# Issuing all output writes of a decode forward-and-backward kernel from SyncE instead of GpSimd

## The chip, the cores and the metric

The kernel runs on one core of a Trainium2 chip. The metric is the device time of one execution in microseconds (us); the engines are named as the profile names them: PE (TensorE matmul), PEld (its weight loads), DVE (VectorE), ACT (ScalarE), POOL (GpSimd) and SP (SyncE). SP computes nothing here; it begins DMA transfers.

## The reference

Two layers, each an attention block over a cached K and V and then an MLP, for one token in each of two batches; then the gradients of nine inputs. Cut to what matters:

```python
def _A_ref(x, k_cache, v_cache, wq, wo):        # x 2x1x1024; caches 2x4x16384x128; 32 query heads
    q = (x @ wq).reshape(B, 1, 32, 128).transpose(0, 2, 1, 3)
    k = jnp.repeat(k_cache, 8, axis=1)
    v = jnp.repeat(v_cache, 8, axis=1)
    p = softmax(einsum("bhqd,bhkd->bhqk", q, k) * 128 ** -0.5)
    return einsum("bhqk,bhkd->bhqd", p, v).transpose(0, 2, 1, 3).reshape(B, 1, 4096) @ wo

def _B_ref(x, w1, b1, w2, b2):                  # w1 1024x3584, w2 3584x1024
    return gelu(layernorm(x) @ w1 + b1) @ w2 + b2

x = A_x
for _ in range(2):
    x = x + _A_ref(layernorm(x), k_cache, v_cache, wq, wo)
    x = x + _B_ref(layernorm(x), w1, b1, w2, b2)
out = x, and the vjp of all this with grad_out: gradients of A_x, k_cache, v_cache, wq, wo, w1, b1, w2, b2
```

All arrays are bf16. The outputs are out_0 (x) and out_1 to out_9 (the gradients); those of the two caches, out_2 and out_3, are 33.5 MB each, and together the outputs are 98.6 MB by the page's account. The two layers share their weights and caches, so each gradient is a sum over both layers.

## The kernel before, in words

The kernel goes once forward through both layers and once back, and streams K, V and the weights from HBM again in every pass: two forward passes of attention (`attn_fwd`) with their MLPs, then MLP and attention backward for layer 1, then the same for layer 0. While attention of layer 0 goes backward (`attn_bwd` with `outputs`, from about 765 us on), the kernel also computes and writes all weight and cache gradients, since only then both layers' terms are known.

**Chunks and slots.** Each piece of data of 1 MiB, loaded or to be written, is a `Chunk`. SBUF has 13 slots for them (plus four borrowed from tiles that are no longer or not yet needed, in earlier stages). `Program.emit` records pieces of work with the chunks that they use; `Program.run` then goes through the pieces in order. Ahead of each piece it gives free slots to the next chunks in the order of their first use, and begins a chunk's load at once; after the last piece that uses a chunk its slot is free. So a slot that gets free goes straight to the next chunk, load or output, and its load stands in SP's instructions at that place, with a wait for whatever last used the slot: for a chunk that was written out, the landing of that write.

The order in which the pieces stand is the order of each engine's instructions; nothing is reordered later. The waits are semaphores. DMAs begun by SP take eight completion semaphores in turn, and each waits for the landing of the eighth before it on the same semaphore; POOL's DMAs have eight of their own.

**Attention backward, steps.** A step s handles 1024 columns of V (`kblock`: DVE transposes a quarter of a chunk, L313, PE multiplies it, L326) and, 16 steps later, the same of K (`direct`, L351: 8 matmuls a step, 32 a chunk). A slope is computed on DVE (L804 to L806), exchanged across partitions by ACT (L360), and the weights wo and wq come in as blocks that PE transposes (L288).

**Outputs.** Of these there are four kinds, each of which begins its write from POOL:
- dK and dV (`kv_outputs`): for each of 8 head groups and 4 column chunks, one chunk for dK (w = 0) and one for dV. PE transposes scores into `blk` (L944), and 8 matmuls with `qm` (L962) fill a PSUM bank each; `cast_out` (L180 on ACT, L183 on DVE, chosen by a running account of both) casts each into the chunk; after the eighth, L967 begins the write of 1 MiB. There are 64 of them.
- weight gradients (`dw_units`, `pieces_rows`): matmuls of rows of two vectors (L1001), again cast by `cast_out`, 8 or 7 to a chunk; L1016 begins the write. There are 31 of these, 23 of 1 MiB and 8 of 896 KB.
- two bias gradients (`dbias`, L1034), of 2 and 7 KB.
- out_0 and out_1 (`col_to_row`, L393), of 4 KB each. out_0 is written in the middle, at 701.9 us; out_1 is the last write of the kernel.

The 31 pieces of weight gradients are spread among the steps by a credit that `outputs` keeps; the last eight, of wq, and some of dK and dV are still to be made when the last load has been issued.

Loads are begun by SP: `ld_kv` (L252, K and V) and `ld_rows` (L257, weights). POOL computes `pow` for the layer norms (L413) in the passes before, and begins two small DMAs at the start.

Of the kernel before, what the change touches and what calls it, by code (L numbers as in the profile page):

```python
# [38 lines left out]
class Program:  # L39
# [11 lines left out]
    def emit(self, fn, uses=()):  # L51
        i = len(self.ops)
        self.ops.append((fn, tuple(uses)))
        for c in uses:
            if c.first is None:
                c.first = i
            c.last = i
# [27 lines left out]
def kernel(  # L85
# [24 lines left out]
    nc = tc.nc  # L110
# [3 lines left out]
    GP = nc.gpsimd  # L114
# [36 lines left out]
    def flat(t):  # L151
        return t.rearrange("p a b -> p (a b)")
# [5 lines left out]
    def ob():  # L158
        st["ob"] += 1
        return obanks[st["ob"] % 3]  # L160


    def load_of(engine, us):
        st[engine] += us
        m = min(st["act"], st["dve"])
        st["act"] = min(st["act"] - m, 2.0)
        st["dve"] = min(st["dve"] - m, 2.0)
# [10 lines left out]
    def cast_out(dst, src):  # L178
        if st["act"] <= st["dve"]:
            S.copy(out=dst, in_=src)  # L180
            load_of("act", 0.67)
        else:
            V.tensor_copy(out=dst, in_=src)  # L183
            load_of("dve", 0.68)

    def dve(us):
        load_of("dve", us)
# [30 lines left out]
    def e_of(l, g):  # L218
        return Et[l][:, g * 1024:(g + 1) * 1024].rearrange("p (a h b) -> p a h b", a=NB, h=8)

    def d_of(l, pos, g):
        t = D1t[:, g * 1024:(g + 1) * 1024] if l == 1 else D0t[:, (pos % 2) * 1024:(pos % 2 + 1) * 1024]
        return t.rearrange("p (a h b) -> p a h b", a=NB, h=8)
# [24 lines left out]
    dKv = out_2.rearrange("b h (p t) d -> (b h) p t d", p=128)  # L248
    dVv = out_3.rearrange("b h (p t) d -> (b h) p t d", p=128)
# [133 lines left out]
    def col_to_row(colT, dram_out):  # L383
        c = P.chunk()

        def f():
            row = c.ap[0:2, 0:D]
            for j0 in range(0, DJ, 4):
                ps = ob()[0:2, :].rearrange("p (a b) -> p a b", a=4)
                for j in range(4):  # L390
                    PE.transpose(ps[:, j, :], colT[:, j0 + j, :], identf[:])
                V.tensor_copy(out=row[:, j0 * 128:(j0 + 4) * 128], in_=flat(ps))
            GP.dma_start(dram_out, row)  # L393

        emit(f, [c])

# [509 lines left out]
    def kv_outputs(pos, g):  # L906

        res = []
        qms = {}

        def rows16():
            ps = ob().bitcast(BF16)[0:16, 0:256].rearrange("p (w d) -> p w d", w=2)
            for w in range(2):
                PE.transpose(ps[:, w, :], qd[:, w, g].rearrange("p l r -> p (l r)"), ident[:])
            r16 = small.tile([16, 2, 128], BF16, name="r16", bufs=2)
            V.tensor_copy(out=r16[:], in_=ps)
            dve(0.35)
            qms["r16"] = r16

        def spread(w, t4):  # L920
            def f():
                if t4 == 0:
                    qms[w] = qmp.tile([128, 8, 128], BF16, name=f"qm{w}")
                ps = ob().rearrange("p (t d) -> p t d", t=4)
                for tl in range(4):
                    PE.matmul(ps[:, tl, :], lhsT=sel8[:, t4 * 4 + tl, :], rhs=qms["r16"][:, w, :], start=True,  # L926
                              stop=True)
                cast_out(qms[w][:, t4 * 4:(t4 + 1) * 4, :], ps)
            return f

        res.append((16, rows16, ()))
        for n, (w, t4) in enumerate([(0, 0), (0, 1), (1, 0), (1, 1)]):
            res.append((17 + n, spread(w, t4), ()))
        for n, (c, w) in enumerate([(c, w) for c in range(NCH) for w in range(2)]):
            stg = P.chunk()
            hold = {}

            def turn(c=c, w=w, hold=hold):
                st["tp"] += 1
                tp = tpb[st["tp"] % 2][:].bitcast(BF16)[:, 0:512].rearrange("p (a b) -> p a b", b=128)  # L940
                for bi in range(4):
                    for l in range(2):
                        src = d_of(l, pos, g) if w == 0 else e_of(l, g)
                        PE.transpose(tp[64 * l:64 * l + 64, bi, :],  # L944
                                     src[:, 4 * c + bi].rearrange("p h b -> p (h b)"), ident[:])
                blk = bkp.tile([128, 4, 128], BF16, name="blk")
                src = tp.rearrange("p a (j t) -> p a j t", j=4)
                dst = blk[:].rearrange("p j (a t) -> p a j t", a=4)
                if st["act"] + 0.36 <= st["dve"] + 0.4:
                    S.copy(out=dst.bitcast(I32), in_=src.bitcast(I32))  # L950
                    load_of("act", 0.36)
                else:
                    V.tensor_copy(out=dst, in_=src)
                    dve(0.4)
                hold["blk"] = blk

            res.append((LAG_O + 2 * n - 2, turn, ()))
            for u in range(8):
                def unit(c=c, w=w, u=u, hold=hold, stg=stg):
                    ps = ob()  # L960
                    j = u // 2
                    PE.matmul(ps, lhsT=hold["blk"][:, j, :],  # L962
                              rhs=flat(qms[w][:, (u % 2) * 4:(u % 2) * 4 + 4, :]), start=True, stop=True)
                    cast_out(stg.ap.rearrange("p (s j q d) -> p s q j d", j=4, q=2, d=128)[
                        :, (u % 2) * 2:(u % 2) * 2 + 2, :, j], ps.rearrange("p (s q d) -> p s q d", q=2, d=128))
                    if u == 7:
                        GP.dma_start((dKv if w == 0 else dVv)[g, :, c * 32:(c + 1) * 32, :],  # L967
                                     stg.ap.rearrange("p (t d) -> p t d", d=128))
                res.append((LAG_O + 2 * n + u // 4, unit, [stg]))
        return res  # L970
# [5 lines left out]
    def row_of(name, c0, n):  # L976
        q, off = ROWS[name]
        return rows[32 * q:32 * q + 4, off + c0:off + c0 + n]
# [29 lines left out]
    def pieces_rows(out_ap, n_in, n_out, c0=0):  # L1008

        rb = max(1, CH // n_out)  # L1010
        res = []
        for j0 in range(0, n_in // 128, rb):
            units = [(j0 + j, c0 + c, 512, j * n_out + c) for j in range(rb) for c in range(0, n_out, 512)]

            def store(ap, j0=j0):
                GP.dma_start(out_ap[j0 * 128:(j0 + rb) * 128, c0:c0 + n_out].rearrange("(j p) n -> p j n", p=128),  # L1016
                             ap[:, 0:rb * n_out].rearrange("p (j n) -> p j n", j=rb))

            res.append((units, store))
        return res  # L1020

    def dbias(yn, n, out_ap):
        q, _ = ROWS[yn]
        c = P.chunk()
        res = []
        for c0 in range(0, n, 512):
            def f(c0=c0):
                ps = ob()[0:1, :]
                PE.matmul(ps, lhsT=ones_bf[32 * q:32 * q + 4, 0:1], rhs=row_of(yn, c0, 512), start=True, stop=True,
                          tile_position=(32 * q, 0))  # L1030
                V.tensor_copy(out=c.ap[0:1, c0:c0 + 512], in_=ps)
                dve(0.6)
                if c0 + 512 >= n:
                    GP.dma_start(out_ap.rearrange("(o f) -> o f", o=1), c.ap[0:1, 0:n])  # L1034
            res.append((f, [c]))
        return res

# [199 lines left out]
```

## Time and profile before

| what | us |
|---|---|
| median of 3 runs | 1311.39 (1309.65 to 1316.94) |
| the profiled execution | 1310.87 |
| its span (first to last instruction) | 1309.1 |
| PE busy | 1006.0 (77%) |
| DVE busy | 794.5 (61%) |
| ACT busy | 585.1 (45%) |
| POOL busy | 64.6 (5%) |
| granted TensorE clock, mean of the span | 0.733 |

The DMA queue of SP moved 364.94 MB in 71.9% of the time of the 16 DMA engines, that of POOL 98.66 MB in 18.9%. From issue to landing (median) a 1 MiB load of V took 16.2 us, of K 13.8, a 1 MiB write 6.3.

How to read it: "busy" is the time in which an engine executes; a wait names the line that ended it. A row of a timeline gives start, duration, engine, line, operation and tiles, and in brackets the idle time before it and what ended that. For DMAs the duration is that of the issue alone; the landing is given apart. In a table of stretches each row has the stretch, its length, the busy us of PE, PEld, DVE, ACT and POOL with their numbers of instructions, the granted clock (1.00 is full speed), the DMA engines' mean busy share and the GB/s moved. The clock that the chip grants PE changes between 1.0 and 0.5 every few tens of us in most of the span.

### The profile page before, as it was taken

The numbers are of one execution on the slowest core, as the hardware profiler recorded it, in microseconds if no ns is written. First come the engines' busy times: TensorE is split into PE (matmuls) and PEld (weight loads), VectorE is DVE, ScalarE is ACT, GpSimd is POOL, SyncE is SP. The second block draws the span as 40 slices with busy tenths as digits, with TensorE's granted clock in tenths as the row PEclk, the third lists the DMA queues.
The fourth block names the chain that finished last, engine by engine and source line by source line (L and its number), as shares of the span: only waits on it lengthen the run. The fifth ranks groups of instructions, "written<-read, shape, count | busy, mean of one in ns | idle before, by whom it ended". The sixth has DMA issues, their size and how long they took to land. (4 is left out here: it accounts for less than half of the span.)

```text
span 1309.1 us, 36548 instructions
## 1 busy us (share of the span) xinstructions
PE 1006.0 (77%) x15785; PEld 727.7 (56%) x15785; DVE 794.5 (61%) x1633; ACT 585.1 (45%) x1462; POOL 64.6 (5%) x115
## 2 busy tenths in 40 slices
PE   4656654878756487777669888888898988898987
PEld 4555554867755487776668865444444444344342
DVE  5766651278765126765644476776667667766575
ACT  0312311213232123555443336867666666757554
POOL 0000000000000000000000000110110001101111
PEclk9999999855555557567658977788677667858575
DMA  9999999999999997999999936899898999988856
GB/s 360 414 414 413 414 414 361 320 341 387 413 413 414 409 383 286 365 412 411 415 411 398 399 122 243 333 377 378 343 358 321 346 343 351 362 324 315 302 200 251
DMA packets 100174, 465.93 MB, mean 356 GB/s; under 512 B 7298, under 2 KB 7298, under 8 KB 60844
## 3 DMA queue, kind: packets, MB, share of 16 engines
q1 hardware_dynamic: 83196, 364.94, 71.9%
q0 software_dynamic: 16816, 98.66, 18.9%
q8 instruction: 123, 2.02, 0.6%
q14 instruction: 39, 0.32, 0.1%
HBM read 364.95 MB, written 98.62 MB: 354 GB/s over the span
## 5 line engine op out<-in xcount | busy, mean ns | idle before, releaser
L313 DVE STREAM_TRANSPOSE kT<-slot 128x512 int32<-128x512 int32 x460 | 310.3, 696 | 121.3 <-PE sc L326 111.0
L326 PE MATMUL sc<-qbd,kT 128*128 128x32 bf16 x4096 | 282.7, 230 | 15.5 <-DVE kT L313 11.4
L326 PEld LDWEIGHTS <-kT 128*128 128x128 bf16 x4096 | 223.8, 121 | 72.3 <-issue 45.7
L351 PEld LDWEIGHTS <-slot 128*128 128x128 bf16 x3680 | 152.4, 105 | 131.8 <-issue 53.8
L351 PE MATMUL sb<-xt,slot 128*128 128x8 bf16 x3680 | 168.7, 177 | 62.9 <-DMA slot<-in_A_v_cache_dram 35.5
L180 ACT CAST slot<-sc 128x512 bf16<-128x512 f32 x303 | 173.6, 588 | 89.5 <-PE sc L962 52.1
L172 ACT COPY kT<-tp 128x512 int32<-128x512 int32 (+1 forms) x165 | 95.9, 582 | 196.0 <-PE tp L288 185.6
L288 PE MATMUL tp<-ident,slot 128*128 128x128 bf16 x1832 | 179.3, 258 | 5.3 <-DVE kT L175 2.1
L183 DVE CAST slot<-sc 128x512 bf16<-128x512 f32 x198 | 134.4, 682 | 65.1 <-PE sc L962 34.2
L962 PE MATMUL sc<-qm,blk 128*128 128x512 bf16 x349 | 158.1, 489 | 14.8 <-ACT slot L180 5.8
L288 PEld LDWEIGHTS <-slot 128*128 128x128 bf16 x1832 | 140.5, 116 | 8.9 <-issue 4.2
L360 ACT COPY xt<-ds 32x64 int32<-32x64 int32 x512 | 123.9, 242 | 30.0 <-DVE ds L806 23.5
L527 ACT ACTIVATE e<-sc 128x512 bf16<-128x512 f32 x32 | 19.0, 597 | 233.8 <-DVE sc L524 198.9
L180 ACT CAST slot<-sb 128x512 bf16<-128x512 f32 x141 | 82.8, 587 | 46.3 <-PE sb L962 27.3
L175 DVE COPY kT<-tp 128x1024 bf16<-128x1024 bf16 (+1 forms) x83 | 53.9, 649 | 81.7 <-PE tp L288 68.9
L183 DVE CAST slot<-sb 128x512 bf16<-128x512 f32 x110 | 75.2, 684 | 34.2 <-PE sb L1001 22.7
L1001 PE MATMUL sc<-rows 4*128 4x512 bf16 x152 | 73.7, 507 | 15.2 <-ACT slot L180 12.1
L962 PE MATMUL sb<-qm,blk 128*128 128x512 bf16 x163 | 78.8, 483 | 4.7 <-ACT slot L180 2.1
L360 ACT COPY xt<-e 32x128 int32<-32x128 int32 x256 | 75.6, 295 | 3.9
L962 PEld LDWEIGHTS <-blk 128*128 128x128 bf16 x512 | 40.4, 105 | 64.6 <-issue 59.8
L967 POOL DMA_DIRECT2D out_dram<-slot x64 | 34.1, 533 | 359.3 <-ACT slot L180 168.5
L1001 PE MATMUL sb<-rows 4*128 4x512 bf16 x88 | 44.6, 507 | 6.8 <-ACT slot L180 4.0
(264 smaller groups left out, 906.0 us busy)
## 6 DMA issues: line engine op xcount, KB each, us to landing
slot<-in_A_v_cache_dram SPq DMA_DIRECT2D x110, 1024.0 KB, 16.2
slot<-in_A_k_cache_dram SPq DMA_DIRECT2D x109, 1024.0 KB, 13.8
out_dram<-slot POOLq DMA_DIRECT2D x87, 1024.0 KB, 6.3
slot<-in_A_wq_dram SPq DMA_DIRECT2D x30, 1024.0 KB, 12.9
slot<-in_A_wo_dram SPq DMA_DIRECT2D x30, 1024.0 KB, 16.5
slot<-in_B_w_dram SPq DMA_DIRECT2D x20, 1024.0 KB, 13.2
slot<-in_B_w_dram SPq DMA_DIRECT2D x20, 896.0 KB, 17.4
ds<-in_A_v_cache_dram SPq DMA_DIRECT2D x8, 1024.0 KB, 16.9
```

The costliest lines, as they stand in the source:

```text
L172: S.copy(out=dst.bitcast(I32), in_=src.bitcast(I32))
L175: V.tensor_copy(out=dst, in_=src)
L180: S.copy(out=dst, in_=src)
L183: V.tensor_copy(out=dst, in_=src)
L288: PE.transpose(tp[:, j, :], t, ident[:])
L313: V.transpose(out=kT[:].bitcast(I32).rearrange("p (w j m) -> p w j m", w=4, j=4), in_=c.ap[:, (i % 4) * 1024:(i % 4 + 1) * 1024].bitcast(I ...
L326: PE.matmul(sc[:, a0:a0 + 4, :, 2 * (i % 4) + q], lhsT=kv[:, 2 * q + w, :, e], rhs=qbd[:, g, 2 * w + e], start=(w == 0 and e == 0), stop=( ...
L351: PE.matmul(acc, lhsT=c.ap[:, n * 128:(n + 1) * 128], rhs=xv[:, i // 4, t // 2, :, 2 * (i % 4) + t % 2], start=(i == 0 and t == 0), stop=( ...
L360: S.copy(out=d[32 * t:32 * t + 32, c0:c0 + cn, j, :], in_=s[32 * j:32 * j + 32, c0:c0 + cn, t, :])
L962: PE.matmul(ps, lhsT=hold["blk"][:, j, :], rhs=flat(qms[w][:, (u % 2) * 4:(u % 2) * 4 + 4, :]), start=True, stop=True)
L967: GP.dma_start((dKv if w == 0 else dVv)[g, :, c * 32:(c + 1) * 32, :], stg.ap.rearrange("p (t d) -> p t d", d=128))
L1001: PE.matmul(ps, lhsT=row_of(xn, j * 128, 128), rhs=row_of(yn, c0, cn), start=True, stop=True, tile_position=(32 * q, 0))
```

## The change

Four lines: the queue on which the output writes are begun. Everything else, the order of the pieces included, is as before. POOL keeps the two small DMAs of the start.

```diff
@@ col_to_row
-            GP.dma_start(dram_out, row)
+            nc.sync.dma_start(dram_out, row)
@@ kv_outputs, after the eighth unit
-                        GP.dma_start((dKv if w == 0 else dVv)[g, :, c * 32:(c + 1) * 32, :],
+                        nc.sync.dma_start((dKv if w == 0 else dVv)[g, :, c * 32:(c + 1) * 32, :],
                                      stg.ap.rearrange("p (t d) -> p t d", d=128))
@@ pieces_rows, store
-                GP.dma_start(out_ap[j0 * 128:(j0 + rb) * 128, c0:c0 + n_out].rearrange("(j p) n -> p j n", p=128),
+                nc.sync.dma_start(out_ap[j0 * 128:(j0 + rb) * 128, c0:c0 + n_out].rearrange("(j p) n -> p j n", p=128),
                              ap[:, 0:rb * n_out].rearrange("p (j n) -> p j n", j=rb))
@@ dbias
-                    GP.dma_start(out_ap.rearrange("(o f) -> o f", o=1), c.ap[0:1, 0:n])
+                    nc.sync.dma_start(out_ap.rearrange("(o f) -> o f", o=1), c.ap[0:1, 0:n])
```

## The prediction

> **What bounds the kernel now.** The change touches 99 output writes; all but one (out_0, begun at 701.93) are begun after 791 us, so I read the page, then the stage from 791 to 1304 alone: its busy times, SP's waits, the chain of waits, and the timelines of SP and POOL. First the chain on the page (shares of the span), and two stretches with the busy us of PE, PEld, DVE, ACT and POOL, then granted clock, DMA share, GB/s:
>
> ```profile
> PE 26%; ACT 7%; DVE 4%; DMA 1%; issue 1%; POOL 0%; POOLq 0%; ACTq 0%; DVEq 0%; SPq 0%
> ```
>
> ```profile
> 100.00:200.00 100.00, 60.10 (x1301) 52.16 (x1301) 58.70 (x121) 27.00 (x82) 0.00 (x0) 1.00 1.02 414
> 840.80:1090.90 250.10, 219.25 (x2253) 116.61 (x2252) 171.78 (x313) 170.07 (x389) 25.38 (x46) 0.75 0.93 351
> ```
>
> The chain names the compute engines and gives DMA 1%. But in the 250 us from 840.8 to 1090.9, where loads and writes run together, two things are nearly full: PE (219 of 250 us, 31 us idle) and the DMA engines (0.93). Compute sets the time there, and DMA stands just behind it. The first row is the rate when loads alone run: 414 GB/s, so 1 MiB takes 2.53 us.
>
> What paces the loads in that stretch (SP's waits: us in total, times, longest):
>
> ```profile
> SPq L252 <- DMA out_dram<-slot: 187.5, 24, 14.2
> SPq L257 <- DMA out_dram<-slot: 31.1, 3, 10.6
> ```
>
> SP stands 219 of 250 us waiting for an output write to land, because the next load goes into the slot that the write empties. Meanwhile POOL goes on and begins further writes. SP and POOL in one such place, and the chain of the same place (start, us, what):
>
> ```profile
> 891.84 0.33 SPq L252 DMA_DIRECT2D slot<-in_A_k_cache_dram  x1
> 903.20 0.33 SPq L252 DMA_DIRECT2D slot<-in_A_v_cache_dram  x1
> 907.22 0.33 SPq L252 DMA_DIRECT2D slot<-in_A_k_cache_dram  x1
> ```
>
> ```profile
> 885.58 0.53 POOL L967 DMA_DIRECT2D out_dram<-slot  x1 [6.51 <-DVE do_raw L741]
> 891.16 0.53 POOL L967 DMA_DIRECT2D out_dram<-slot  x1 [5.05 <-ACT slot L180]
> 895.24 0.76 POOL L1016 DMA_DIRECT2D out_dram<-slot  x1 [3.54 <-DVE slot L183]
> 898.01 0.53 POOL L967 DMA_DIRECT2D out_dram<-slot  x1 [2.01 <-ACT kT L172]
> ```
>
> ```profile
> 885.58 6.15 DMA out_dram<-slot
> ...
> 891.84 13.27 DMA slot<-in_A_k_cache_dram
> ```
>
> Each load of the first fence was released by the landing of a write of the second: 885.58 frees the load at 891.84, 891.16 the one at 903.20, 895.24 the one at 907.22. While SP waited, two or three more writes were on their way, so the DMA engines had work. The third fence is the one place of the stretch where the chain runs through DMA: the write takes 6.15 us to land, the load 13.27, and PE's L351 then starts.
>
> **What the change does to the order.** The instruction order of PE, DVE and ACT is the same; POOL loses 99 DMAs and SP goes from 354 to 453. In SP's new order a write stands where its last cast is emitted, and the load into its slot mostly stands right behind it: write 885.58, load 891.84, write 891.16, load 903.20, write 895.24, load 907.22, write 898.01. So the write of 898.01, ready 9.2 us before the load of 907.22, must now wait until that load is issued. Going through the stage with the recorded issue times, 30 of 99 writes have such a later load ahead of them; they come to 97 us, 3.2 us each, before any of it feeds back. No load has a write ahead of it that was issued later than itself, so loads lose nothing directly.
>
> The larger effect is on the DMA engines. When SP waits for the landing of the DMA that it issued last, nothing of its queue is left to move, and POOL's queue, which filled this gap, is gone. What one such gap costs, from transfers that ran alone (a write on POOL near the end, then a load on SP at 769.4; us from issue to landing):
>
> ```profile
> DMA to landing us min/median/max: 4.6/4.6/4.6
> ```
>
> ```profile
> DMA to landing us min/median/max: 5.0/5.0/5.0
> ```
>
> Less the 2.53 us in which 1 MiB moves, that is 2.05 and 2.45 us in which nothing moves. A write on SP is not in this trace, and the gap in question is the end of a write and the start of a load, so I take the middle, 2.25, and keep both ends.
>
> **The sum.** From the load of 840.8 up to the load of 1090.9 SP's new order holds 47 writes and 43 loads, 92.3 MB, and 28 of the loads stand directly behind the write of their own slot.
> - Moving: at the loads-only 414 GB/s 223 us; at the mixed rate of the row above, 351/0.93 = 377, 245 us. One queue is like the first row, half of it writes like the second; I take 400: 231 us.
> - Gaps: 28 x 2.25 = 63 us (57 to 69).
> - Together 294 us for what takes 250 now: 44 us too much (30 to 64).
> - Lead: the stretch's 18 K loads are issued 10.9 to 33.9 us, median 18.3, before the first L351 matmul that reads them (SP's issue against every 32nd L351). A load alone needs 5.0, so 13 us of lateness is used up once, before PE waits (6 at the tightest): 44 - 13 = **31 us**; ends 30 - 13 = 17 and 64 - 6 = 58.
> - Other stages: 11 more such loads, 25 us of gaps, lie before 840 and after 1090.9, where the DMA share is 0.59 (764 to 830) and 0.87 (1090.9 to 1250, 21 us idle). I count them at nothing; uncovered, they are the 25 us.
> - out_0: a 4 KB write at 701.9 that now stands behind four loads (issued 702.0 to 704.6, landing 13.5 to 17.5 us later); the next load, issued at 707.0, waits for it until about 722, one gap of 2.25 us. Its cover is that the first weight block of this stage lands at 694.9 and is read from 700.5, 5.6 us later. Zero; 2 us without that cover.
> - SP issues 99 more DMAs at 0.33 to 0.50 us, 33 to 50 us spread over waits of 219 in the stretch alone: inside them. POOL gets back 0.53 to 0.76 us each and has nothing waiting for it: zero.
> - All DMAs of SP take eight completion semaphores in turn and wait for the landing of the eighth before. Loads and writes now share them; a queue that drains every 90/28 = 3.2 DMAs is never eight deep: zero.
> - The last writes (from 1280.47) have no load between them and land 4.6 us after issue; on SP the issue is shorter by up to 0.4 us: zero.
>
> The profiled execution took 1310.87 us (its span 1309.1 and 1.8 around it), 0.5 under the median of 1311.39. 1310.9 + 31 = 1342.
>
> **Rivals.**
> 1. No change. PE is idle 31 us of the stretch, and if the late loads fall into that idle time, the 31 us vanish: 1311, up to 1317. For it: DMA has 1% of the chain. Against it: PE's idle time is many short waits (PEld before L962 waits 126 times in the whole span, 2.5 us at most), and a late load comes on top of those instead of replacing them. The Trainium skill (DMA: Bandwidth & Descriptors, section "Issuing engines are not separate DMA queues") says that DMAs of all issuing engines run on the same 16 engines, and that issuing from several saves only sequencer time; by that rule this would be the result. The trace speaks against it in this kernel, since POOL's writes at 895.24 and 898.01 were begun while SP stood waiting.
> 2. Faster. In one queue a write and its load no longer share the engines with others: in the stretch writes land after 8.0 us (median of L967) and loads after 7.4 (L252), alone after 4.6 and 5.0, 5.8 us less for a pair; the DMA piece of the chain, 6.15 + 13.27, would shrink to 9.6, 10 us less: 1301. It decides as long as a write is held up on SP by less than 5.8 us; the first count (3.2 us for 30 of 99) is below that, which is why it has a chance, but the 294 us against 250 say that the delays add up.
> 3. Much slower. Late writes also keep back the casts of the next tenant of a slot, and the 25 us of the other stages are not covered: 1342 + 25 and more, from 1367 on to about 1395.
> 4. That the writes don't move is excluded by the instruction order.
>
> **Chances.** The forecast's case 0.66 (1328 to 1369), no change 0.13, faster 0.09, much slower 0.12. A measurement of this kernel tells about 0.5%, 6.6 us, from no change. Faster 0.09, same 0.13, slower 0.78. The range takes in the no-change case and the start of the third rival: 1308 to 1376.
>
> **What would show it.** In the profile after: DMA's share between 840 and 1090 falls below 0.93 with GB/s near or below 310; SP still waits for writes, but each wait is a landing of 4.6 to 7.5 us; writes wait on SP behind loads; PE's L351 waits for K loads, which it does for 1.3 us now; and the added time lies between 850 and 1250, with the last 50 us as long as before. It is wrong if mixed transfers in one queue run nearer to 414 GB/s and the gaps near 2 us (then 17), or if the granted clock rises as PE idles: 0.01 of it is worth 219 x 0.01/0.75 = 2.9 us in the stretch.

## The result, and the profile after

The changed kernel takes 1400.09 us (median of 4 runs, 1395.53 to 1402.18), beside 1310.52 of the kernel before on the same chip: a ratio of 1.0676, with a 95% interval from 1.0621 to 1.0731. That is 90 us slower by the medians and 89 by the ratio, the figure used below, where 31 were forecast, and above the range of 1308 to 1376. The profiled execution has a span of 1399.4 us (before 1309.1) at a mean granted clock of 0.706 (before 0.733).

The chain of waits on the page, the line that showed DMA at 1% before:

```profile
PE 21%; DMA 15%; ACT 4%; DVE 3%; issue 1%; SPq 0%; ACTq 0%; DVEq 0%
DMA out_dram<-slot 12%; PE sc L962 5%; DMA slot<-in_A_k_cache_dram 3%; PE sc L1001 3%; ACT xt L360 2%; PE sb L962 2%; PE tp L288 2%; PE sb L1001 2%; PE sc L326 2%; ACT slot L180 2%; PE tp L944 1%; PE sb L351 1%; DVE slot L183 1%; DVE kT L313 0%; PE sc L926 0%
```

DMA is now 15% of the chain, 12% of it the landing of output writes. Four stretches of the kernel after (start and end, length, busy us of PE, PEld, DVE, ACT and POOL, granted clock, DMA share, GB/s):

```profile
764.00:836.60 72.60, 61.09 (x694) 36.53 (x696) 52.40 (x97) 45.77 (x112) 0.00 (x0) 0.76 0.63 232
836.60:1165.80 329.20, 236.36 (x2331) 123.41 (x2333) 180.43 (x326) 178.83 (x408) 0.00 (x0) 0.69 0.78 267
1165.80:1340.00 174.20, 143.71 (x1116) 63.33 (x1116) 100.62 (x164) 98.84 (x217) 0.00 (x0) 0.60 0.83 305
1340.00:1399.00 59.00, 51.12 (x269) 20.34 (x268) 36.02 (x68) 29.25 (x51) 0.00 (x0) 0.56 0.56 215
```

The second row runs between the same two load instructions that enclosed the prediction's stretch, and so does the same work: 329.2 us in place of 250.1, 79 more. The DMA engines are busy 0.78 of it at 267 GB/s (before 0.93 and 351). PE works 236 us of it and stands still for 93, where it stood for 31. What SP waits for in this stretch (us in total, times, longest), and the three longest waits of the compute engines:

```profile
SPq L252 <- DMA out_dram<-slot: 251.8, 24, 14.6
SPq L257 <- DMA out_dram<-slot: 34.0, 4, 9.7
```

```profile
PEld L351 <- DMA slot<-in_A_k_cache_dram: 66.3, 12, 13.1
ACT slot L180 <- PE sc L962: 62.9, 55, 13.0
PE sb L351 <- DMA slot<-in_A_k_cache_dram: 57.7, 12, 12.6
```

The first two lines hold 28 waits, one for each load that stands right behind the write of its own slot. Before, SP waited there for much the same share of the stretch (219 of 250 us, now 286 of 329), while POOL's writes moved. The difference is in the last fence: PE's L351 and its weight loads, which run beside each other, wait 12 times for a K load, 66 and 58 us. Before, that wait was this:

```profile
PEld L351 <- DMA slot<-in_A_k_cache_dram: 1.3, 2, 1.2
```

One such place, on SP (start, us of the issue, what) and in the chain of waits of the same 20 us:

```profile
1042.67 0.34 SPq L252 DMA_DIRECT2D slot<-in_A_v_cache_dram  x1
1043.11 0.37 SPq L967 DMA_DIRECT2D out_dram<-slot  x1
1051.27 0.34 SPq L252 DMA_DIRECT2D slot<-in_A_k_cache_dram  x1
1051.72 0.37 SPq L967 DMA_DIRECT2D out_dram<-slot  x1
1060.03 0.39 SPq L257 DMA_DIRECT2D slot<-in_A_wq_dram  x1
```

```profile
1043.11 8.14 DMA out_dram<-slot
...
1051.27 6.23 DMA slot<-in_A_k_cache_dram
...
1057.55 0.39 PE sb L351 x8
```

SP issues a load and a write, and then nothing until that write has landed 8.14 us later, because the next load goes into its slot. From 1042.67 to 1051.27 to 1060.03 a round of 2 MiB takes 8.60 and 8.76 us; moving 2 MiB at the prediction's 2.53 would take 5.06. On POOL, the writes would have been begun meanwhile.

### The profile page after: what moved, and what is told of

Same layout as the page of the kernel before. It is cut to its first block, busy times and chain, and to the rows that moved or that the text cites. A ratio compares the mean times of both kernels' runs of the same rounds, so it can differ in the third digit from the quotient of the medians.

```text
span 1399.4 us, 36420 instructions
## 1 busy us (share of the span) xinstructions
PE 1027.5 (73%) x15778; PEld 736.2 (53%) x15785; DVE 796.7 (57%) x1633; ACT 586.9 (42%) x1462; POOL 6.5 (0%) x16
## 5 line engine op out<-in xcount | busy, mean ns | idle before, releaser
L326 PE MATMUL sc<-qbd,kT 128*128 128x32 bf16 x4096 | 286.3, 232 | 15.1 <-DVE kT L313 11.1
L326 PEld LDWEIGHTS <-kT 128*128 128x128 bf16 x4096 | 227.3, 122 | 73.4 <-issue 47.3
L351 PE MATMUL sb<-xt,slot 128*128 128x8 bf16 x3680 | 169.1, 177 | 131.2 <-DMA slot<-in_A_k_cache_dram 92.4
L351 PEld LDWEIGHTS <-slot 128*128 128x128 bf16 x3680 | 151.9, 106 | 206.2 <-DMA slot<-in_A_k_cache_dram 106.1
L180 ACT CAST slot<-sc 128x512 bf16<-128x512 f32 x303 | 174.1, 588 | 148.4 <-PE sc L962 99.0
L183 DVE CAST slot<-sc 128x512 bf16<-128x512 f32 x198 | 134.6, 684 | 124.5 <-PE sc L962 88.8
L288 PE MATMUL tp<-ident,slot 128*128 128x128 bf16 x1832 | 185.6, 264 | 6.5 <-DVE kT L175 3.0
L962 PE MATMUL sc<-qm,blk 128*128 128x512 bf16 x346 | 164.6, 515 | 17.5 <-ACT slot L180 8.2
L288 PEld LDWEIGHTS <-slot 128*128 128x128 bf16 x1832 | 145.1, 119 | 9.8 <-issue 5.5
L180 ACT CAST slot<-sb 128x512 bf16<-128x512 f32 x141 | 82.8, 588 | 76.2 <-PE sb L962 49.3
L183 DVE CAST slot<-sb 128x512 bf16<-128x512 f32 x110 | 75.4, 685 | 47.8 <-PE sb L1001 22.5
L1001 PE MATMUL sc<-rows 4*128 4x512 bf16 x152 | 76.8, 531 | 16.7 <-ACT slot L180 12.8
L1001 PEld LDWEIGHTS <-rows 4*128 4x128 bf16 x240 | 22.0, 102 | 40.1 <-issue 30.5
## 6 DMA issues: line engine op xcount, KB each, us to landing
slot<-in_B_w_dram SPq DMA_DIRECT2D x20, 896.0 KB, 17.4
```

What stands on the lines that cost most here:

```text
L288: PE.transpose(tp[:, j, :], t, ident[:])
L326: PE.matmul(sc[:, a0:a0 + 4, :, 2 * (i % 4) + q], lhsT=kv[:, 2 * q + w, :, e], rhs=qbd[:, g, 2 * w + e], start=(w == 0 and e == 0), stop=( ...
L351: PE.matmul(acc, lhsT=c.ap[:, n * 128:(n + 1) * 128], rhs=xv[:, i // 4, t // 2, :, 2 * (i % 4) + t % 2], start=(i == 0 and t == 0), stop=( ...
L962: PE.matmul(ps, lhsT=hold["blk"][:, j, :], rhs=flat(qms[w][:, (u % 2) * 4:(u % 2) * 4 + 4, :]), start=True, stop=True)
L1001: PE.matmul(ps, lhsT=row_of(xn, j * 128, 128), rhs=row_of(yn, c0, cn), start=True, stop=True, tile_position=(32 * q, 0))
```

## The experiments

Theories. **Drained queue**: each load right behind the write of its own slot lets SP's queue run empty, and the restart costs time in which nothing moves. **One queue**: loads and writes slow each other when they share a queue. **Late casts**: SP, standing at a write until the chunk's last cast is done, holds back the loads behind it. A third rival says that writes through a queue of SP's kind are slow by themselves.

### The transfers by themselves

A kernel with nothing but 1 MiB transfers, 12 slots and eight of each kind, each group ended by a wait for all (`i` numbers the slots; loads alone and writes alone are groups of one kind):

```python
for i in range(8): store(i); load(i)            # D: all on SP
for i in range(8): store(i, GP); load(i)        # E: writes on POOL
for i in range(8): store(i); load(i + 8)        # F: load into the slot written four writes before
for i in range(8): store(i + 1); load(i)        # H: load into the slot of the write before
```

G is F with the writes on POOL.

> This kernel computes nothing of the reference: it only loads 1 MiB pieces of K into 12 slots and writes slots out, in stretches of 8 transfers (24 for loads alone) with a full stop between them: loads alone; writes alone on SP, then on POOL; D: write, then the load of its own slot, all on SP; E: the same with the writes on POOL; F: write, then the load of the slot written four writes before, all on SP; G: the same with the writes on POOL; H: write, then the load of the slot of the write before it, all on SP. Theory (a load right behind the write of its slot drains SP's queue, and starting it again costs about 4 us): a pair in D takes 8.7 to 9.5 us, in E, F and G 5.1 to 5.8, in H 5.1 to 6.5. Rival one queue (reads and writes slow each other down in one queue, dependent or not): F and H take as long as D, 8 us or more, G and E 5.1 to 5.8. The prediction's figures for D would be 2 x 2.62 + 2.25 = 7.5 us.

Measured, per MiB: loads alone 2.49 us, writes alone 2.49 on SP and 2.50 on POOL. Per pair of write and load: D 8.84 (8.6 to 9.0), E, F and G 4.9, H 4.91; D is within what the drained queue expected, the others are just below it. Two MiB at 2.49 are 4.98, so D's gap is 3.86 us a pair, and the others have none. D, and below it H, on SP's timeline:

```profile
153.20 0.34 SPq L72 DMA_DIRECT2D slot<-in_A_k_cache_dram  x1
154.01 0.33 SPq L77 DMA_DIRECT2D out_dram<-slot  x1
161.79 0.34 SPq L72 DMA_DIRECT2D slot<-in_A_k_cache_dram  x1
162.23 0.38 SPq L77 DMA_DIRECT2D out_dram<-slot  x1
170.59 0.34 SPq L72 DMA_DIRECT2D slot<-in_A_k_cache_dram  x1
```

```profile
353.63 0.33 SPq L72 DMA_DIRECT2D slot<-in_A_k_cache_dram  x1
354.01 0.54 SPq L77 DMA_DIRECT2D out_dram<-slot  x1
358.53 0.33 SPq L72 DMA_DIRECT2D slot<-in_A_k_cache_dram  x1
358.91 0.53 SPq L77 DMA_DIRECT2D out_dram<-slot  x1
363.47 0.33 SPq L72 DMA_DIRECT2D slot<-in_A_k_cache_dram  x1
```

Loads follow each other at 8.59 and 8.80 us in D, at 4.90 and 4.94 in H; the difference is that in H a load and one more write stand in the queue behind the write that is waited for. D's rounds are as long as those of the kernel after (8.60, 8.76). One queue falls, and so do slow writes on SP, for writes of the dK and dV kind: F and H run in one queue at full rate.

### The writes stay on SP, the slots come free one write later

The kernel after, but a written chunk's slot is handed on only when the next write has been emitted. No load then stands right behind the write of its own slot; the queues are as after.

```diff
+HOLD = 1
...
                 if c.last == i:
-                    free.append(c.slot)
+                    if c.load is None:
+                        held.append(c.slot)
+                        if len(held) > HOLD:
+                            free.append(held.pop(0))
+                    else:
+                        free.append(c.slot)
```

> The changed kernel, but a slot that was written out is given to the next chunk only after the next write has been begun, so that no load stands right behind the write of its own slot (39 did). All writes stay on SP. Theory (the drained queue): with another write in the queue while a load waits, most of the added 89 us goes: 1310 to 1340 us. Rival one queue (loads and writes of one queue slow each other): stays at 1390 to 1410. Rival late casts (SP stands at a write until its casts are done and holds back the loads behind it): loads come later still, 1400 or more.

Measured 1314.32 us (10 runs), ratio to before 0.998 (0.9939 to 1.0021). All 89 us are gone with every write still on SP. Its row for 840.8 to 1090.9, columns as above, and SP's waits there (its lines are numbered 7 higher: L974 is the write L967, L259 the load L252, L190 the cast L183):

```profile
840.80:1090.90 250.10, 221.84 (x2215) 117.47 (x2219) 168.98 (x306) 167.50 (x378) 0.00 (x0) 0.71 0.91 347
```

```profile
SPq L974 <- DVE slot L190: 131.8, 31, 9.5
SPq L259 <- DMA out_dram<-slot: 41.9, 15, 7.2
```

PE works 222 us of the 250 and DMA has a share of 0.91, close to before (219 and 0.93). SP now stands 132 us at writes that wait for their last cast, and the time is none the worse, which speaks against late casts. So does the kernel after itself: in its stretch of 329 us SP's waits for casts come to less than 10 us. And since the weight gradients are written through SP's queue here too, slow writes on SP fall for them as well.

The same later reuse on the kernel before, with the writes on POOL, shows what it does by itself:

> The kernel before (writes on POOL) with the same later reuse of written slots; it tells what holding one slot back costs or brings by itself. Theory (the drained queue) and both rivals: within 10 us of the kernel before, 1300 to 1320 us; a little faster if SP's waits for landings cost anything before.

Measured 1306.02, ratio 0.9956 (0.9914 to 0.9998). So with the later reuse SP and POOL as the writes' queue differ by 0.2% by their ratios (0.6% by their medians); both intervals lie within 1% of the kernel before. With two writes held (`HOLD = 2`), also on POOL:

> The kernel before, writes on POOL, with written slots reused two writes later. SP then hardly waits for landings, but two of 13 slots are always held back. Holding one back gave 0.9956 of the kernel before (0.9914 to 0.9998). Theory: SP's waits for landings cost nothing before, since POOL filled them, so no further gain: 1298 to 1318 us; if fewer slots in use cost more than the waits, 1320 or more.

Measured 1318.11, ratio 1.0044 (1.0016 to 1.0072): nothing is won by more.

### SP waits for the casts, POOL still writes

The kernel before, and at the place of each big write SP copies partition 0 of the finished chunk (8 KB) to a scratch array, 95 copies. SP then stands at the casts where the change makes it stand, but the 1 MiB writes are POOL's.

```diff
+    def sp_mark(ap, n):
+        nc.sync.dma_start(marks_d.pop()[:, 0:n], ap[0:1, 0:n])
...
+                        sp_mark(stg.ap, CH)
                         GP.dma_start((dKv if w == 0 else dVv)[g, :, c * 32:(c + 1) * 32, :],
```

> The kernel before with its writes on POOL, and at the place of 95 of them an added DMA of SP that copies 8 KB of the finished chunk to a scratch buffer: SP then stands at each write's place until its casts are done, as in the changed kernel, but the 1 MiB writes keep POOL's queue. Theory (the drained queue): the writes of POOL go on filling the gaps, within 10 us of the kernel before, 1302 to 1322 us. Rival late casts (SP's standing at the casts holds back loads): most of the 89 us come back, 1370 or more.

Measured 1325.01, ratio 1.014 (1.0079 to 1.02), just above what was expected. If the two costs simply add up, late casts have at most 14 of the 89 us, and the copies' own cost is in these 14.

### Where the gaps cost: late reuse in one part alone

The later reuse again on the kernel after, but only for the 9th to 55th write (the gaps that are left lie outside the stretch, 12 with out_0's), or only from the 56th on (30 are left, 28 of them in the stretch). The second has `56 <= written < 200` in these lines:

```diff
...
+                    if c.load is None:
+                        held.append(c.slot)
+                        written += 1
+                        if not 9 <= written < 56 or len(held) > 1:
+                            free.append(held.pop(0))
+                        if not 9 <= written < 56:
+                            free.extend(held)
+                            held.clear()
...
```

> The changed kernel with the later reuse of written slots for writes 9 to 55 only (the stretch that was 840 to 1091 us before): of 39 loads right behind the write of their slot 12 are left, 10 of them late in the stage. Theory (each such load costs about 4 us of DMA time, and the stage's DMA engines have no room): 1312 plus about 27, 1330 to 1350 us. The prediction's item that the gaps of the other stages cost nothing: 1305 to 1322. Rival late casts and rival one queue: 1385 or more.

> The changed kernel with the later reuse from write 56 on only: 30 such loads are left, 28 of them in the stretch that was 840 to 1091 us. Theory: 28 x 3.87 us of gaps and the moving at 2.49 us per MiB are 327 us for 250, less 14 us of lead: 1312 plus about 63, 1365 to 1385 us. By the prediction's gap of 2.25 us: 1335 to 1350. Rivals late casts and one queue: 1385 or more.

Measured 1329.44, ratio 1.0178 (1.0116 to 1.024), for the first, slightly under what was expected, and 1383.69, ratio 1.0568 (1.0513 to 1.0624), for the second, within it. The gaps of the stretch cost 73 us, those outside 19 (medians, against 1310.68 on the same chip); together 92, beside 89 measured.

### Which writes

Only the 64 writes of dK and dV on SP (27 loads right behind their write), and only the 31 weight-gradient writes (11 such loads); the other writes stay on POOL. The edit of the kernel after, for the first at L1016 (and likewise L393 and L1034), for the second the same at L967 (and L393 and L1034):

```diff
-                nc.sync.dma_start(out_ap[j0 * 128:(j0 + rb) * 128, c0:c0 + n_out].rearrange("(j p) n -> p j n", p=128),
+                GP.dma_start(out_ap[j0 * 128:(j0 + rb) * 128, c0:c0 + n_out].rearrange("(j p) n -> p j n", p=128),
```

> Only the 64 writes of dK and dV are begun by SP, the 35 others stay on POOL: 27 of the 39 loads right behind the write of their slot are left. Theory (the drained queue): a gap of SP's queue costs only where the other queue has nothing to move, and POOL's 31 writes of 1 MiB or less fill part of them, so less than the share by number (89 x 27/38 = 63): 1320 to 1360 us. If each such load costs the same whatever POOL does: 1365 to 1385. By bytes in the shared queue (rival one queue): 89 x 64/95 = 60, 1372.

> Only the 31 writes of weight gradients are begun by SP, the 64 of dK and dV and the small ones stay on POOL: 11 of the 39 loads right behind the write of their slot are left. Theory: POOL's 64 writes fill nearly all gaps, within 12 us of the kernel before, 1300 to 1324 us. If each such load costs the same whatever POOL does: 89 x 11/38 = 26, 1330 to 1345.

Measured 1354.06, ratio 1.0316 (1.0252 to 1.038), and 1313.37, ratio 1.0005 (0.9969 to 1.0042). By number of such loads their shares of 89 us would be 62 and 25; measured are 40 and none (medians against 1313.7). Both are within what the drained queue expected, but they don't show that POOL's writes fill gaps of SP's queue, because the first gaps are free in any case. Moving the 92.3 MB of the stretch at 2.49 us per MiB takes 219 of its 250 us, and 13 us of lateness stay hidden (the prediction's lead). Of the 28 gaps there, 20 stand behind writes of dK and dV, 7 behind weight gradients and 1 behind a bias gradient (SP's order in the trace of the kernel after). Without any filling the first run would be 219 + 20 x 3.86 - 250 - 13 = 33 us slower by the stretch, and some 12 more by its 7 gaps outside; for the second, 219 + 7 x 3.86 = 246 is less than the 250 that the stretch takes anyway. That is near 40 and none too.

### The writes on ACT's queue

As after, with `nc.scalar.dma_start` at all four places: a queue beside SP's, issued by another engine.

> All output writes begun from ACT's queue in place of SP's or POOL's. Theory (the drained queue) and rival late casts: SP's order and queue are as in the kernel before and another queue holds the writes, so 1305 to 1330 us (ACT now waits for DVE's casts ahead of each write). Rival one queue: the same, since the writes have a queue of their own. A third rival, writes begun by hardware queues (packets of 2 KB where POOL's have 4 KB) are slower by themselves: 1350 or more.

Measured 1348.81, ratio 1.0266 (1.0225 to 1.0308), outside what was expected of the drained queue and next to what the third rival expected. The writes alone were no slower through SP's queue than through POOL's (2.49 and 2.50), and with the later reuse all writes went through SP's queue at 0.998 of before, so they needn't be slow here. What the trace shows instead is ACT's sequencer at the write, from 843 to 1084 us (ns min/median/max):

```profile
L967 ACTq EVENT_SEMAPHORE  x30: 82/1150/2089, 843.0 to 1084.3; - x30
```

ACT stands a median of 1.15 us, 30 times, until DVE's casts of the chunk are done, and can run no cast of its own meanwhile. 30 times 1.15 is 35 us, about what this kernel is slower (1348.81 against 1312.01 on the same chip). That the one makes the other is not shown, and the same trace has a rival. From 764 us to the end, before and with ACT's queue (columns as above):

```profile
764.00:1309.00 545.00, 474.18 (x4481) 239.00 (x4478) 370.57 (x656) 351.52 (x785) 57.48 (x98) 0.72 0.83 313
764.00:1344.70 580.70, 501.00 (x4422) 246.10 (x4426) 371.08 (x652) 351.38 (x785) 0.00 (x0) 0.66 0.78 294
```

PE is busy 27 us longer for the same work, at a granted clock of 0.66 in place of 0.72, and idle only 9 us longer (79.7, before 70.8). If the waits for casts were the whole cause, the added time should be idle time of PE. How much of the 36 us belongs to the clock and how much to the waits, and whether the one brings the other, is open.

### Why a restart costs 3.9 us and not 2.25

Once more transfers alone, in rounds that each start from an empty queue, since the first transfer of a round needs the slot of the last one before:

```python
for i in range(9): load(i); load(i + 1)         # J
for i in range(9): load(i); store(i + 1)        # K
for i in range(9): store(i); load(i + 1)        # L
for i in range(0, 18, 2): load(i); store(i + 1); store(i + 2)   # M
for i in range(0, 18, 2): load(i); load(i + 1); store(i + 2)    # N
```

> Computes nothing of the reference: groups of 1 MiB transfers, all on SP, each group begun when the last transfer of the group before has landed. J: two loads; K: a load and a write; L: a write and a load; M: a load and two writes; N: two loads and a write. The first run of this kind gave 2.49 us a MiB in a filled queue and 8.8 us for K, 1.6 more than a lone start (4.6) and one MiB. If any restart costs that: J 8.7, K 8.8, L 8.7. If it comes only of a load and a write starting together: J 7.1, K 8.8, L 8.7 or so. If only of a write behind a load: J and L 7.1, K 8.8. M and N one MiB more than K, 11.3, in each case.

Measured per round: J 7.1 us, K 8.8, L 7.3, M and N 11.25, the third of the cases expected. Less 2.49 per MiB the gaps are 2.1 (J), 3.8 (K), 2.3 (L) and 3.8 (M and N). K, then L, then N on SP:

```profile
106.48 0.33 SPq L72 DMA_DIRECT2D slot<-in_A_k_cache_dram  x1
106.86 0.42 SPq L77 DMA_DIRECT2D out_dram<-slot  x1
115.28 0.33 SPq L72 DMA_DIRECT2D slot<-in_A_k_cache_dram  x1
115.65 0.42 SPq L77 DMA_DIRECT2D out_dram<-slot  x1
124.04 0.33 SPq L72 DMA_DIRECT2D slot<-in_A_k_cache_dram  x1
```

```profile
185.08 0.34 SPq L77 DMA_DIRECT2D out_dram<-slot  x1
185.47 0.42 SPq L72 DMA_DIRECT2D slot<-in_A_k_cache_dram  x1
192.42 0.33 SPq L77 DMA_DIRECT2D out_dram<-slot  x1
192.80 0.42 SPq L72 DMA_DIRECT2D slot<-in_A_k_cache_dram  x1
199.70 0.33 SPq L77 DMA_DIRECT2D out_dram<-slot  x1
```

```profile
357.06 0.80 SPq L72 DMA_DIRECT2D slot<-in_A_k_cache_dram  x2
357.96 0.38 SPq L77 DMA_DIRECT2D out_dram<-slot  x1
368.30 0.80 SPq L72 DMA_DIRECT2D slot<-in_A_k_cache_dram  x2
```

The prediction's 2.25 is the gap of J and L. In the rounds that have a load with a write right behind it (K, M and N), 1.6 us come on top, and it is that load that lands late. In K and M it is the first, which lands after 6.2 to 6.5 us in place of J's 4.5 to 4.8. In N the first load lands after 4.5 to 4.7 us as in J, and the second, ahead of the write, after 8.2 to 8.5 in place of 6.6 to 6.9. In the kernel after every restart of the stretch has such a load: in 19 of 28 the first, as in K and M, in 9 the second, as in N. In a queue that is never empty (F and H above) the same order of load and write costs nothing. What makes these 1.6 us is open.

## Why the prediction was wrong in its size

The direction and the mechanism hold: later reuse alone, with all writes still on SP, takes the time back to 0.998 of before. Point by point:

- **Gaps, "28 x 2.25 = 63 us (57 to 69)": the step that failed.** The count of 28 is right, as SP's 28 waits show. One gap measures 3.86 us in D (3.8 in K, M and N), and in the kernel after a round with one load and one write is as long as there. 28 x 3.86 is 108 us, 45 more than forecast. Both bounds came from transfers alone on the chip, 2.05 from a write and 2.45 from a load; neither row has a restart in which a write stands right behind a load, and the bounds were taken as if the nearest rows enclosed every case.
- **Moving, "I take 400: 231 us".** Also off, the other way: 92.3 MB at 2.49 us per MiB (421 GB/s) are 219 us, 12 less. Loads and writes in one queue run at the rate of loads alone; the 377 GB/s, a row's GB/s divided by its DMA share, was no rate of mixed transfers, since E and G, loads on SP and writes on POOL, also take 4.9 us a pair. By luck this error hid 12 us of the other. 219 + 108 = 327, beside 329 measured for the stretch.
- **Lead, "13 us of lateness is used up once": right.** The stretch is 79 us longer, and began 4 us earlier than before. The work at its end is 61 to 65 us late (the same casts of ACT and DVE, before and after); 79 - 4 - 13 = 62.
- **Other stages, "I count them at nothing": wrong.** After 1165.8 a further 27 to 31 us are lost, nearly all of them between 1235 and 1300; the run with the gaps left only outside the stretch is 19 us slower. The 0.87 of DMA share beside them was not the room that it was taken for: once the loads are late, nothing gives the time back. (PE's idle time in that row is 159.1 - 140.9 = 18 us, not 21.) The forecast named 25 us for the case that they are not covered.
- In all: 31 forecast, + 45 for the gaps, - 12 for the moving, + 27 for the other stages is 91, beside 89.
- **Counted at zero and found so:** out_0 (the next load waited from 703.8 to 716.6 as described, and the work behind it was not late), the issues on SP (with the later reuse all 99 are there, at 0.998), and the last writes (a median of 4.2 us from issue to landing, and the last 59 us longer by 1 to 2). In the stretch nothing in SP's waits points to the eight semaphores.
- **Rival 1, no change:** its condition was that late loads fall into PE's 31 us of idle time. They did not: PE's standing rose from 31 to 93 us, in waits of up to 13. The Trainium skill (DMA: Bandwidth & Descriptors, section "Issuing engines are not separate DMA queues") states that beginning DMAs from several engines saves only the sequencer's time for it. With the later reuse this agrees, SP and POOL differing by 0.2%; in the kernel as it was changed the issuing engine decided over 6.8%, by the waits that stand ahead of its next DMA.
- **Rival 2, faster:** loads in the stretch do land sooner (median of L252 7.4, now 6.2 us), but writes later (L967 8.0, now 11.2). A pair takes 17.4 in place of 15.4, so its condition, a shorter pair, was not met.
- **Rival 3, much slower,** had 0.12 and named the sum that comes nearest (1367 to 1395), by one of its two causes: the gaps of the other stages do cost. Its other cause, late writes that keep back the casts of a slot's next tenant, is small: in the stretch such casts wait for a landing 6 us in all (ACT's L180 3.4, DVE's L183 1.6 and L1031 1.2). That it comes near is mostly luck, since 45 of the 58 us that the forecast lacked are the mis-sized gap, which this rival doesn't name.
- **Signs.** DMA share 0.78 and 267 GB/s (forecast: below 0.93, near or below 310), PE waiting for K loads, added time between 850 and 1250: as named. SP's waits were to be landings of 4.6 to 7.5 us; they are up to 14.6, a mean of 10.2 (285.8 us in 28). The clock fell (0.733 to 0.706) where a rise was named as a risk. In the stretch PE's idle time grew by 62 us and its busy time by 17 for the same work. The sum for the DMAs, 327 of 329 us, accounts for the stretch without the clock; what the lower clock costs by itself was not measured.

## What to carry to other kernels

Before two streams of DMAs are put into one queue, look for a DMA that waits for the one issued just ahead of it: each such place lets the queue run empty, and the price is measured by the transfers in that very order, not by one alone. If the streams have to share a queue, hand a written buffer on one write later: in H and in this kernel that took the whole cost away. The queue of another engine hides the gaps too: POOL, which has next to nothing else to do here, did so in the kernel before, while ACT, which has casts to run, ended 2.7% slower, for a reason that is open.

## What the runs showed of the hardware that was not expected

- Loads and writes in turn, in one queue that is kept filled, move 1 MiB in 2.45 us (4.9 a pair), no slower than either alone (2.49).
- A queue that starts from empty loses 2.1 to 2.3 us, but 3.8 to 3.9 when a write stands right behind a load in what restarts it; that load lands 1.6 us late. Why is open.
- Reuse of a slot one write later, so that a load and a write stand behind the write that is waited for, takes a 3.86 us gap to nothing (D against H).
